# Attention sums in one step a pair, numerators and denominators as 32-column products

## The chip, the cores and the metric

The program runs on one core of one Trainium2 chip. The metric is the device time of one execution in microseconds; the kernel before has a median of 1244.84 us over three runs (1244.61 to 1248.21).

## What is computed

Attention with random features over 8 batches, 8 heads, 576 tokens and 64 dimensions, and then a gated feed-forward layer over the 4608 tokens (512 to 1536 and back to 512). Cut to what matters here:

```python
proj = einsum('bhsd,df->bhsf', x, w_phi)              # 64 -> 128 features, for q and for k
proj = proj - max(abs(proj), axis=-1, keepdims=True)
q_p, k_p = concatenate([exp(proj), exp(-proj)])       # 256 features a token
kv  = einsum('bhsf,bhsd->bhfd', k_p, v)               # sums over keys
z   = sum(k_p, axis=2)
num = einsum('bhsf,bhfd->bhsd', q_p, kv)              # numerators
den = einsum('bhsf,bhf->bhs', q_p, z)[..., None] + 1e-06
attn = num / den
out  = (silu(x @ w_gate) * (x @ w_val)) @ w_out       # x is attn, heads side by side
```

## The kernel before

Two heads make a pair; there are 32 pairs (8 batches of 4). A pair's keys are projected in three groups (`GROUPS`: two, two and one tile of 128 tokens; the last tile holds the 64 left-over tokens of both heads). For each group PE writes the projections into a PSUM bank, DVE takes the largest absolute value (L449) and subtracts it (L454) into a buffer `kp`, and ACT makes exp(x) and exp(-x) of it (L458, L459). Then PE sums over the keys (L472): the exponentials are the stationary operand, 64 features at a time into the upper or the lower half of the partitions of the bank `ps_kv`, and the values with two columns of ones (66 columns, `D2`) are the moving one. The three groups share two buffers of `kp`, and each group has a step of its own on PE. ACT copies `ps_kv` into `kvs` (L494) so that for each head a block of 128 columns holds 64 columns of kv and 64 equal columns of z.

Queries get their exponentials the same way, turned so that features lie on the partitions: in the first 8 pairs (`EARLY_PAIRS`) by products with the identity (L535), later by transposes on DVE. The numerators are four steps a pair, one for each head and half of the tokens: two products of 128x128 by 128x288 (`kvs` by exp(q) and by exp(-q)) into one bank, recorded under L313, the line of a helper through which most products go. 64 partitions of the bank hold the numerators and the other 64 the denominator, repeated. ACT copies the first into `num` (L622) and the second, plus 1e-6, into `den` (L624). DVE transposes `den` in blocks of 32 (L631), takes the reciprocal of one column of each block (L632), transposes it back, spread (L633), and multiplies (L635). The result goes on to the feed-forward layer on chip, or to `x_dram`.

The feed-forward products (L313 into `gv` and `o`, later L1008) take 12 chunks of 384 tokens. All products are float32 or split into a high and a low part of type fp32r. The last six chunks go in pairs by a scheme with seven products in place of eight, whose combined weights POOL makes (L915, L920).

The order of the instructions on each engine is not written by hand. Every step is handed to a planner (`Plan`) with its engine, a cost, a rank and what it waits for; the planner plays them through and issues them in that order. Attention steps have the better ranks, feed-forward products come last on PE and fill what is left. A step that needs a PSUM bank (`take`) starts only when one of two work banks is free (in the early pairs three more); `give` returns it. While the first feed-forward product has not begun, or a sum is open, the planner puts filler products where PE would have nothing (`nothing`, L1092 and L1096). Each engine then works strictly in that order.

## Time and profile before

| | |
|---|---|
| median of three runs | 1244.84 us |
| the profiled execution | 1244.83 us, span 1243.0 us, clock 0.998 |
| PE busy | 1215.6 us (98%) |
| DVE busy | 940.5 us (76%) |
| ACT busy | 686.3 us (55%) |
| POOL busy | 241.8 us (19%) |

One execution was recorded. Times in the profile's rows are in microseconds, unless a row says mean ns. PE is the matrix engine's products and PEld its weight loads, which overlap them; DVE, ACT and POOL are the vector, scalar and general engines. A row of groups reads: line, engine, operation, output and input tile, sizes, count, then busy time, mean ns of one, and the idle time just before them with what ended it. Busy times of PE overlap each other. A float32 product of the program appears as two records on PE. The early pairs run from 0 to some 130 us, the other 24 from about 300 to 705 us, beside feed-forward products; from about 810 us on the paired chunks run.

### The profile page before, as it was taken

The page shows a single profiled execution, that of the slowest core. Times are in us where ns is not written, and L with a number is a line of the kernel's source. Part 1 is how long each engine was busy: PE and PEld are TensorE (multiplying, and loading weights), DVE is VectorE, ACT ScalarE, POOL GpSimd, SP SyncE. Part 2 cuts the span into 40 slices and gives each one's busy share as a digit, 9 for nine tenths or more (in the row PEclk, how much of TensorE's full clock was granted, in tenths as well). Part 3 has the DMA queues.
Part 4 walks back from the last instruction along what each step waited for, and adds up shares of the span by engine and source line. Part 5 has one row for each costly group of instructions (what it writes and reads, how often), then busy time and mean ns, then how long its engine had stood idle before and what let it go on. Part 6 is the DMA issues. An engine that isn't in the chain of part 4 may idle for free.

```text
span 1243.0 us, 21611 instructions
## 1 busy us (share of the span) xinstructions
PE 1215.6 (98%) x8160; PEld 1087.3 (87%) x8160; DVE 940.5 (76%) x1674; ACT 686.3 (55%) x1419; POOL 241.8 (19%) x306
## 2 busy tenths in 40 slices
PE   8999999999999999999999999989999999999998
PEld 7777899999888888888888899979998899989997
DVE  7998799998899899999999632575658655675553
ACT  6887333336888787887887521333335433453333
POOL 0000000000000000000000010066555655565550
PEclk9999999999999999999999999999999999999999
DMA  4433444447554443444533254632223312222211
GB/s 141 137 120 98 146 178 169 174 168 219 168 159 130 130 114 110 119 123 124 152 113 97 77 189 140 190 113 66 77 73 109 124 57 72 77 102 77 77 51 51
DMA packets 107321, 149.40 MB, mean 120 GB/s; under 512 B 52048, under 2 KB 61776, under 8 KB 107216
## 3 DMA queue, kind: packets, MB, share of 16 engines
q1 hardware_dynamic: 106752, 147.76, 37.4%
q8 instruction: 64, 1.05, 0.3%
q14 instruction: 41, 0.34, 0.1%
q10 hardware_dynamic: 464, 0.26, 0.1%
HBM read 119.67 MB, written 28.31 MB: 119 GB/s over the span
## 4 chain that ended last, share of the span: by engine, by line
PE 84%; DVE 9%; DMA 3%; ACT 2%; POOL 1%; issue 1%; SPq 0%; DVEq 0%; ACTq 0%; POOLq 0%
PE gv L313 22%; PE gv L1008 19%; PE o L313 19%; PE work L313 16%; PE kv L472 5%; PE kv L313 2%; DVE m L454 1%; DVE km L449 1%; POOL a L915 1%; POOL a L920 1%; DMA w_lo<-wlo_dram 1%; DVE xl L957 1%; DVE m L953 1%; DVE m L593 0%; DVE m L633 0%
## 5 line engine op out<-in xcount | busy, mean ns | idle before, releaser
L313 PE MATMUL gv<-xh,w_hi 128*128 128x384 f32 x576 | 200.6, 348 | 2.4 <-DVE th L744 1.4
L313 PE MATMUL gv<-xh,w_lo 128*128 128x384 f32 x576 | 193.3, 336 | 0.0
L313 PE MATMUL gv<-xl,w_hi 128*128 128x384 f32 x576 | 193.2, 335 | 0.0
L1008 PE MATMUL gv<-xh,m 128*128 128x384 f32 x504 | 151.0, 338 | 3.4 <-ACT m L1016 2.6
L915 POOL TENSOR_TENSOR a<-w_hi,m 128x256 f32<-128x256 f32 x48 | 40.3, 870 | 485.5 <-DMA m<-wlo_dram 477.8
L915 POOL TENSOR_TENSOR a<-w_hi,w_lo 128x256 f32<-128x256 f32 x96 | 85.8, 924 | 192.9 <-DMA w_lo<-wlo_dram 176.0
L920 POOL TENSOR_TENSOR a<-a 128x256 f32<-128x256 f32 x144 | 115.2, 800 | 8.5
L313 PEld LDWEIGHTS gv<-xh,w_hi 128*128 128x128 f32 x576 | 108.3, 188 | 6.7 <-DVE th L744 2.0
L1019 DVE TENSOR_TENSOR a<-gv,a 128x384 f32<-128x384 f32 x72 | 39.9, 554 | 95.3 <-PE gv L1008 95.1
L313 PE MATMUL work<-m,m 128*128 128x288 f32 x408 | 110.6, 408 | 0.7 <-ACT m L624 0.7
L313 PE MATMUL o<-w_hi,hh 128*128 128x512 f32 x270 | 111.1, 411 | 0.0
L313 PEld LDWEIGHTS gv<-xl,w_hi 128*128 128x128 f32 x576 | 108.3, 188 | 3.1 <-DVE xl L659 0.2
L313 PEld LDWEIGHTS gv<-xh,w_lo 128*128 128x128 f32 x576 | 108.1, 188 | 0.0
L313 PE MATMUL o<-w_hi,hl 128*128 128x512 f32 x270 | 106.7, 395 | 0.0
L1008 PEld LDWEIGHTS gv<-xh,m 128*128 128x128 f32 x504 | 93.5, 189 | 6.4 <-ACT m L1016 3.2
L313 PE MATMUL o<-w_lo,hh 128*128 128x512 f32 x243 | 95.6, 393 | 0.0
L313 PEld LDWEIGHTS work<-m,m 128*128 128x128 f32 x408 | 75.5, 189 | 19.0 <-ACT m L624 1.0
L742 ACT ACTIVATE th<-gv 128x384 f32<-128x384 f32 x72 | 35.4, 491 | 99.5 <-PE gv L313 96.7
L767 ACT CAST hh<-th 128x384 fp32r<-128x384 f32 x108 | 55.2, 511 | 51.9 <-DVE th L747 39.4
L1008 PE MATMUL gv<-xh,w_hi 128*128 128x384 f32 x216 | 72.8, 337 | 5.0 <-DVE a L1019 5.0
L744 DVE SCALAR_TENSOR_TENSOR th<-th,gv 128x384 f32<-128x384 f32 x72 | 39.5, 548 | 46.1 <-ACT th L742 45.5
L768 DVE TENSOR_TENSOR hl<-th,hh 128x384 fp32r<-128x384 f32 x108 | 66.5, 618 | 8.7 <-ACT hh L767 8.4
(179 smaller groups left out, 2927.7 us busy)
## 6 DMA issues: line engine op xcount, KB each, us to landing
w_lo<-wlo_dram SPq DMA_DIRECT2D x60, 512.0 KB, 3.6
w_lo<-wlo_dram SPq DMA_DIRECT2D x78, 256.0 KB, 3.0
wlo_dram<-w_lo SPq DMA_DIRECT2D x36, 256.0 KB, 2.0
out_dram<-osb SPq DMA_DIRECT2D x30, 256.0 KB, 2.9
a<-in_wg_dram SPq DMA_DIRECT2D x12, 512.0 KB, 3.3
a<-in_wv_dram SPq DMA_DIRECT2D x12, 512.0 KB, 3.2
a<-in_wo_dram SPq DMA_DIRECT2D x12, 512.0 KB, 3.2
m<-wlo_dram SPq DMA_DIRECT2D x12, 512.0 KB, 3.6
```

The lines of the kernel that those rows point to most:

```text
L313: nc.tensor.matmul(o, l, r, start=a, stop=z)
L449: kmax = add("DVE", dve(n * NF), lambda m=m, view=view: vec.tensor_reduce(out=m, in_=view(), axis=AX.X, op=ALU.max, apply_absolute_value=T ...
L454: vec.tensor_tensor(out=room[:, :, 1], in0=view(), op=ALU.subtract, in1=m.rearrange("p (n o) -> p n o", o=1).broadcast_to([P, n, NF]))
L472: nc.tensor.matmul(ps_kv[r, n:n + (2 if tail else 1) * D2], x[:, r], y, start=t + h + k == 0, stop=tail and k == 1)
L742: s1 = add("ACT", act(CH), lambda: nc.scalar.activation(t_, ps_gv[0][:, :CH], AF.Tanh, scale=0.5), [ends[0], th_free[j]], FIRST)
L744: s2 = add("DVE", dve(CH), lambda: nc.vector.scalar_tensor_tensor(out=t_, in0=t_, scalar=1.0, in1=ps_gv[0][:, :CH], op0=ALU.add, op1=ALU.m ...
L767: s4 = add("ACT", act(CH), lambda: nc.scalar.copy(get(hh[b]), th[j]), [made, hid_free[b]], FIRST)
L768: s5 = add("DVE", dve(CH), lambda: nc.vector.tensor_tensor(out=get(hl[b]), in0=th[j], in1=get(hh[b]), op=ALU.subtract), [s4], FIRST)
L915: gp.tensor_tensor(out=full()[:, block(n)], in0=hi[:, block(n)], in1=get(low)[:, block(n)], op=ALU.add)
L920: gp.tensor_tensor(out=x[:, block(o)], in0=x[:, block(l)], in1=x[:, block(r)], op=ALU.subtract)
L1008: nc.tensor.matmul(o[:, :CH], l, r, start=begin and i == 0, stop=i == len(terms) - 1, skip_group_check=True)
L1019: return add("DVE", dve(CH), lambda: vec.tensor_tensor(out=snap[n](), in0=bank_c[:, :CH], in1=snap[n](), op=ALU.add), after, FIRST)
```

## The change

Sums over keys: the values get one column of ones (65 columns). Each group of exponentials has its own buffer, so that all three of a pair stand side by side; a pair's sums are one step on PE, after the last exponentials, in place of three. The projections of the next pair's keys wait for that step. `kvs` holds for each of the four blocks 64 columns of kv and 32 equal columns of z (`KV`).

Numerators and denominators: one step a pair that takes two banks. The stationary operand has 32 columns, and four products write the four 32-partition strips of a bank. In the first bank, strip n holds dimensions 32(n mod 2) and on of head n div 2 for the first 512 tokens. In the second bank are the same for the last 64 tokens, and beside them the denominators: strip n holds those of head n div 2 for one half of the tokens (288). ACT then makes three copies a pair in place of eight. DVE transposes 288 columns of denominators in place of 576 and takes nine reciprocals a partition; POOL spreads them in six copies to the partitions where the numerators stand (`spread_out`), and the transpose back (now L657) and the product (L659) follow as before. The step that used to wait for the store of the previous pair's result was the copy on ACT; now the step on PE waits for it. The planner counts several banks for a step, and holds other steps that want a bank while one waits for two.

The core of the diff (left out: the lines that only put the name of a bank into a list, and some that rename):

```diff
-D2 = D + 2
+D2 = D + 1
+KV = D + 32
...
-                if s.take is not None and not self.free and not (s.early and self.extra):
+                if s.take is not None and (saved or len(s.take) > len(self.free) + (len(self.extra) if s.early else 0)):
                     held.append((key, s))
+                    saved = True
...
-            if s.take is not None:
-                self.bank[s.take] = (self.extra if s.early and self.extra else self.free).pop(0)
+            for t in s.take or ():
+                self.bank[t] = (self.extra if s.early and self.extra else self.free).pop(0)
...
+STRIPS = 350
...
-    kp = [view("m1", [2, 2, 2, NF]) for _ in range(2)]
-    kvs = [view("m2", [4 * P]) for _ in range(2)]
+    kp = [view("m1", [n, 2, NF]) for n in (4, 4, 1)]
+    kvs = [view("m2", [4 * KV]) for _ in range(2)]
...
-    rc = sb("rc", [P, NBL])
+    rc, rp = sb("rc", [P, NBL]), sb("rp", [P, NBL // 2])
...
-            kproj = add("PE", w * (pe32(width) if plain else 3 * pe(width)), project, k_ready, rk, take=key)
+            kproj = add("PE", w * (pe32(width) if plain else 3 * pe(width)), project,
+                        [*k_ready, last.get(("kv", i - 1))], rk, take=[key])
...
-            ksub = add("DVE", dve(n * NF), centre, [kmax, last.get(("kp", 3 * i + g - 2))], freeing, give=key)
+            ksub = add("DVE", dve(n * NF), centre, [kmax], freeing, give=key)
...
-            def values(t0=t0, t1=t1, room=room, tail=tail):
-                kv_open[0] = not tail
+            powers.append(e1)
+        def values():
+            for g, (t0, t1) in enumerate(GROUPS):
+                tail = t1 == 5
                 for t in range(t0, t1):
                     for h in range(1 if tail else 2):
                         for k in range(2):
-                            x = room[:, 2 * (t - t0) + h, k]
+                            x = kp[g][:, 2 * (t - t0) + h, k]
                             y = get(vf[one])[:, 4].rearrange("p h d -> p (h d)") if tail else get(vf[one])[:, t, h]
                             n = (2 * k + h) * D2
                             for r in (slice(0, P // 2), slice(P // 2, P)):
                                 nc.tensor.matmul(ps_kv[r, n:n + (2 if tail else 1) * D2], x[:, r], y,
                                                  start=t + h + k == 0, stop=tail and k == 1)
-            kv = add("PE", 2 * n * pe32(D2), values, [e1, *v_in, last.get(("kv", i - 1)), *kv_steps[-1:]], rk)
-            last["kp", 3 * i + g] = kv
-            kv_steps.append(kv)
+        kv = add("PE", 20 * pe32(D2) // 2 + STRIPS, values, [*powers, *v_in, last.get(("kvc", i - 1))], rk)
+        last["kv", i] = kv
...
-            kvc.append(add("ACT", act(4 * D), lambda ones=ones: nc.scalar.copy(
-                cut(kvs[j], ones), sums(ones)), [kv_steps[-1], *use("kvs")], rank))
-        last["kv", i] = kvc[-1]
+            def out_of_bank(ones=ones):
+                x = ps_kv[:, :4 * D2].rearrange("p (n d) -> p n d", d=D2)
+                o = kvs[j].rearrange("p (n d) -> p n d", d=KV)
+                if ones:
+                    nc.scalar.copy(o[:, :, D:], x[:, :, D:D + 1].broadcast_to([P, 4, KV - D]))
+                else:
+                    nc.scalar.copy(o[:, :, :D], x[:, :, :D])
+            kvc.append(add("ACT", act(4 * (KV - D if ones else D)), out_of_bank, [kv, *use("kvs")], rank))
+        last["kvc", i] = kvc[-1]
...
-        copied, nu = [], None
-        for h in range(2):
-            for part in range(2):
-                key = ("n", i, h, part)
-                c = slice(part * SH, (part + 1) * SH)
-                ra, rb = rows(h)
-                def numerators(key=key, h=h, c=c):
-                    o = work[plan.bank[key]][:, :SH]
-                    terms = []
-                    for k in range(2):
-                        n = slice((2 * k + h) * P, (2 * k + h + 1) * P)
-                        terms.append((kvs[j][:, n], (qe, qx)[k][j][:, h, c]))
-                    matmuls([(o, l, r, m == 0, m == len(terms) - 1) for m, (l, r) in enumerate(terms)])
-                nu = add("PE", 2 * pe32(SH), numerators, [*done[h], *kvc, nu], rn, take=key)
-                free = last.get(("num", i - 1), ())
-                copied.append(add("ACT", act(SH), lambda key=key, ra=ra, c=c: nc.scalar.copy(
-                    num[ra, c], work[plan.bank[key]][ra, :SH]), [nu, *free], freeing))
-                copied.append(add("ACT", act(SH), lambda key=key, ra=ra, rb=rb, c=c: nc.scalar.activation(
-                    den[ra, c], work[plan.bank[key]][rb, :SH], AF.Copy, bias=1e-6), [nu, *free], freeing, give=key))
+        free = last.get(("num", i - 1), ())
+        keys = [("n", i, n) for n in range(2)]
+        WIDE = 4 * P
+        def numerators():
+            oa, ob = (work[plan.bank[key]] for key in keys)
+            strips = lambda o, c, l, x, n, begin, final: nc.tensor.matmul(
+                o[32 * n:32 * n + 32, c], l, x, start=begin, stop=final)
+            for k in range(2):
+                for n in range(4):
+                    at = (2 * k + n // 2) * KV + 32 * (n % 2)
+                    strips(oa, slice(0, WIDE), kvs[j][:, at:at + 32], (qe, qx)[k][j][:, n // 2, :WIDE],
+                           n, k == 0, k == 1)
+            for k in range(2):
+                for n in range(4):
+                    at = (2 * k + n // 2) * KV + 32 * (n % 2)
+                    strips(ob, slice(SH, SH + S - WIDE), kvs[j][:, at:at + 32], (qe, qx)[k][j][:, n // 2, WIDE:],
+                           n, k == 0, False)
+                for n in range(4):
+                    at = (2 * k + n // 2) * KV + D
+                    strips(ob, slice(0, SH), kvs[j][:, at:at + 32],
+                           (qe, qx)[k][j][:, n // 2, (n % 2) * SH:(n % 2 + 1) * SH], n, False, k == 1)
+        nu = add("PE", pe32(WIDE) * 2 + pe32(SH) * 2 + 300 + STRIPS, numerators, [*done[0], *done[1], *kvc, *free], rn, take=keys)
+        c_den = add("ACT", act(SH), lambda: nc.scalar.activation(
+            den[:, :SH], work[plan.bank[keys[1]]][:, :SH], AF.Copy, bias=1e-6), [nu], freeing)
+        c_num = [add("ACT", act(S - WIDE), lambda: nc.scalar.copy(
+            num[:, WIDE:], work[plan.bank[keys[1]]][:, SH:SH + S - WIDE]), [nu], freeing, give=keys[1])]
+        c_num.append(add("ACT", act(WIDE), lambda: nc.scalar.copy(num[:, :WIDE], work[plan.bank[keys[0]]]), [nu], freeing, give=keys[0]))
         last["kvs", i] = last["nu", i] = nu
-        turned = qe[j][:, 0]
+        turned = qe[j][:, 0, :SH]
         wide = lambda t: t.rearrange("p (a j) -> p a j", j=32)
-        t0 = add("DVE", dve(S), lambda: vec.transpose(turned, den), [*copied, *done[0], *done[1]], rt)
-        t1 = add("DVE", 260, lambda: vec.reciprocal(rc, wide(turned)[:, :, 0]), [t0], rt)
+        half = NBL // 2
+        t0 = add("DVE", dve(SH), lambda: vec.transpose(turned, den[:, :SH]), [c_den], rt)
+        t1 = add("DVE", 210, lambda: vec.reciprocal(rp, wide(turned)[:, :, 0]), [t0, last.get(("rc", i - 1))], rt)
+        def spread_out():
+            for u in range(2):
+                nc.gpsimd.tensor_copy(rc[:, u * half:(u + 1) * half], rp)
+            for h in range(2):
+                for u in range(2):
+                    n = 32 * (2 * h + u)
+                    r = 32 * (2 * h + 1 - u)
+                    nc.gpsimd.tensor_copy(rc[r:r + 32, u * half:(u + 1) * half], rp[n:n + 32])
+        ts = add("POOL", 6 * 230, spread_out, [t1, last.get(("num'", i - 1))], rt)
+        last["rc", i] = ts
         t2 = add("DVE", dve(S), lambda: vec.transpose(
-            wide(den), rc.rearrange("p (a o) -> p a o", o=1).broadcast_to([P, NBL, 32])), [t1], rt)
-        t3 = add("DVE", dve(S), lambda: vec.tensor_tensor(out=num, in0=num, in1=den, op=ALU.mult), [t2], rt)
+            wide(den), rc.rearrange("p (a o) -> p a o", o=1).broadcast_to([P, NBL, 32])), [ts], rt)
+        t3 = add("DVE", dve(S), lambda: vec.tensor_tensor(out=num, in0=num, in1=den, op=ALU.mult), [t2, *c_num], rt)
+        last["num'", i] = t2
```

How the order changes. PE at an early pair, from the numerators on; `o` and `work` are banks, `kv` the bank of the sums, `ident` the products that turn the next queries. Before:

```order
L313 MATMUL o_126<-m_0_104,m_0_105 128x288 x2
L313 MATMUL o_128<-m_0_104,m_0_105 128x288 x2
L313 MATMUL work_132<-m_0_104,m_0_105 128x288 x2
L313 MATMUL o_127<-m_0_104,m_0_105 128x288 x2
L472 MATMUL kv<-m_0_105,m_0_104 64x66 x16
L535 MATMUL o_126<-ident,m_0_105 128x128 x4
L472 MATMUL kv<-m_0_105,m_0_104 64x66 x16
L313 MATMUL o_128<-wbd,m_0_105 128x256 x2
```

Now:

```order
L614 MATMUL o_127<-m_0_104,m_0_105 32x512 x8
L614 MATMUL work_134<-m_0_104,m_0_105 32x64 x4
L614 MATMUL work_134<-m_0_104,m_0_105 32x288 x4
L614 MATMUL work_134<-m_0_104,m_0_105 32x64 x4
L614 MATMUL work_134<-m_0_104,m_0_105 32x288 x4
L478 MATMUL kv<-m_0_105,m_0_104 64x65 x32
L478 MATMUL kv<-m_0_105,m_0_104 64x130 x4
L538 MATMUL o_129<-ident,m_0_105 128x128 x4
```

Four wide steps have become one of 24 narrow products, and the three pieces of sums, which other products parted, stand together behind it.

PE at the sums of the last pair, among feed-forward products (`o` with 512 columns). Before:

```order
L313 MATMUL o_126<-w_hi_87,hl_121 128x512
L472 MATMUL kv<-a_1_2616,m_0_104 64x66 x32
L313 MATMUL o_127<-w_hi_87,hh_119 128x512
L313 MATMUL o_127<-w_lo_97,hh_119 128x512
L313 MATMUL o_127<-w_hi_87,hl_121 128x512
L472 MATMUL kv<-a_1_2616,m_0_104 64x132 x4
L313 MATMUL o_128<-w_hi_87,hh_119 128x512
```

Now:

```order
L316 MATMUL o_127<-w_hi_86,hl_121 128x512
L478 MATMUL kv<-a_1_2767,m_0_104 64x65 x32
L478 MATMUL kv<-a_1_2767,m_0_104 64x130 x4
L316 MATMUL o_128<-w_hi_86,hh_119 128x512
L316 MATMUL o_128<-w_lo_96,hh_119 128x512
```

Over all pairs the sums stood in 85 such pieces before and stand in 32 now. Behind the last numerators there were 551 feed-forward products ahead of the first paired chunk (L1008 before, L1033 now); now there are 194. Filler products ahead of the first feed-forward product number 40 in place of 26.

DVE at the denominators of a late pair; `rc` and `rp` hold reciprocals, `km` and `work` belong to the keys of another pair, `th` and `gv` to the feed-forward layer. Before:

```order
L631 STREAM_TRANSPOSE m_0_104<-m_0_105 128x576
L449 TENSOR_REDUCE km_108<-work_133 128x4
L454 TENSOR_TENSOR m_0_104<-work_133,km_108 128x4x128
L449 TENSOR_REDUCE km_109<-work_132 128x4
L454 TENSOR_TENSOR m_0_104<-work_132,km_109 128x4x128
L449 TENSOR_REDUCE km_106<-work_133 128x1
L632 RECIPROCAL rc<-m_0_104 128x18
L633 STREAM_TRANSPOSE m_0_105<-rc 128x576
L635 TENSOR_TENSOR m_0_105<-m_0_105 128x576
```

Now:

```order
L643 STREAM_TRANSPOSE m_0_104<-m_0_105 128x288
L644 RECIPROCAL rp<-m_0_104 128x9
L452 TENSOR_REDUCE km_106<-work_133 128x1
L457 TENSOR_TENSOR m_0_104<-work_133,km_106 128x128
L769 SCALAR_TENSOR_TENSOR th_117<-th_117,gv_130 128x384
L657 STREAM_TRANSPOSE m_0_105<-rc 128x576
L659 TENSOR_TENSOR m_0_105<-m_0_105 128x576
```

Between the reciprocal and the transpose back, where nearly nothing stood, there are now mostly three to ten instructions of other work, while POOL spreads the reciprocals; at three pairs there are none or one.

More of the change, by code (lines that the diff above doesn't have):

```diff
@@ L535, in turn @@
                             nc.tensor.transpose(o[:, (h * w + t) * P:(h * w + t + 1) * P], y[:, 2 * t + h], ident)
-                tn = add("PE", u * 108, turn, [qc], rank, take=key2)
+                tn = add("PE", u * 108, turn, [qc], rank, take=[key2])
                 last["qy", n] = tn
@@ L564, in project @@
                         matmuls([(acc, wst_hi, x, True, False), (acc, wst_lo, x, False, True)])
[L566 removed]
+                    pj = add("PE", 2 * pe(SH), project, [lo], rq, take=[key])
                     copies.append(add("ACT", act(SH), lambda h=h, c=c, key=key: nc.scalar.copy(
```

22 lines of the change are left out of this document (6 added, 16 removed).

## The prediction

> **What bounds the kernel now.** I first read the page's busy times and chain, then the table by stage, then the waits inside the attention stage, and last the order of time on PE, for the price of a single product. All come from one profiled execution: 1244.83 us, of which the span is 1243.0. The median of the runs shown is 1244.84 us, so the sum below is made against 1244.8.
>
> The page's busy times and the engines of its chain of waits, then the table by stage:
>
> ```profile
> PE 1215.6 (98%) x8160; PEld 1087.3 (87%) x8160; DVE 940.5 (76%) x1674; ACT 686.3 (55%) x1419; POOL 241.8 (19%) x306
> PE 84%; DVE 9%; DMA 3%; ACT 2%; POOL 1%; issue 1%; SPq 0%; DVEq 0%; ACTq 0%; POOLq 0%
> ```
> ```profile
> 150.00:300.00 150.00, 150.00 (x832) 145.08 (x831) 137.69 (x264) 59.82 (x110) 0.59 (x5) 1.00 0.52 182
> 300.00:705.00 405.00, 400.18 (x3411) 341.13 (x3410) 374.12 (x716) 321.18 (x702) 0.00 (x0) 1.00 0.43 127
> 705.00:810.00 105.00, 105.00 (x549) 97.70 (x548) 39.65 (x64) 27.69 (x52) 9.98 (x13) 1.00 0.51 165
> ```
>
> In the second fence the columns are the stretch, its length, the busy time of PE, PEld, DVE, ACT and POOL, the granted clock, the DMA share and GB/s. From 300 to 705 us 24 of the 32 pairs run among the feed-forward products; PE works 400.18 of 405 us, at full clock. DVE is not far behind with 374.12 (92%), so I ask whether anything makes PE wait there:
>
> ```profile
> PE work L313 <- ACT m L624: 2.3, 2, 1.6
> PE work L313 <- DVE a L554: 1.3, 3, 0.7
> PE kv L472 <- ACT m L458: 0.5, 1, 0.5
> PE work L313 <- DVE m L454: 0.2, 1, 0.2
> ```
>
> Those are all of PE's waits in the 405 us, 4.3 us together. From 705 to 810 us PE still works through products of the last chunk without a break while DVE is idle for 65 us. So the feed-forward work is a reserve that fills PE whenever attention is late: time saved on PE is time saved, as long as that reserve lasts.
>
> **What an attention product costs.** Busy times of PE overlap, so I take distances between starts. In order of time, on PE, at an early and at a late pair (start, us from first start to last end, what, count):
>
> ```profile
> 33.59 2.10 PE L313 MATMUL o<-m,m 128*128 128x288 f32 x8
> 35.53 1.13 PE L313 MATMUL work<-m,m 128*128 128x288 f32 x4
> ...
> 39.23 1.16 PE L472 MATMUL kv<-m,m 128*64 128x66 f32 x32
> 40.32 1.13 PE L313 MATMUL o<-wbd,m 128*128 128x256 f32 x4
> ...
> 42.46 0.67 PE L472 MATMUL kv<-m,m 128*64 128x132 f32 x8
> 43.06 1.13 PE L313 MATMUL work<-wbd,m 128*128 128x256 f32 x4
> ```
> ```profile
> 678.02 0.34 PE L313 MATMUL gv<-xh,w_lo 128*128 128x384 f32 x1
> 678.20 0.39 PE L313 MATMUL o<-w_hi,hh 128*128 128x512 f32 x1
> 678.43 0.39 PE L313 MATMUL o<-w_lo,hh 128*128 128x512 f32 x1
> 678.66 0.40 PE L313 MATMUL o<-w_hi,hl 128*128 128x512 f32 x1
> 678.99 2.09 PE L472 MATMUL kv<-m,m 128*64 128x66 f32 x64
> 681.01 0.50 PE L313 MATMUL o<-w_hi,hh 128*128 128x512 f32 x1
> 681.34 0.39 PE L313 MATMUL o<-w_lo,hh 128*128 128x512 f32 x1
> ```
>
> A float32 product of the program shows as two records. Numerators (L313, 288 columns): eight records take 35.53 - 33.59 = 1.94 us, 0.2425 each, 0.84 ns a column. Eight products a pair are 16 records: **3.88 us a pair**.
>
> The sums over keys (L472) use 64-column weights in the two halves of the array. 32 records take 1.09 us (40.32 - 39.23) and 64 take 2.02 (681.01 - 678.99); the extra 32 cost 0.93, so two records together take 0.058 us. One alone would need 66 x 0.84 = 0.055, so the two halves run side by side. 16 such waves are 0.93, which leaves 0.16 us of the 1.09 as an edge inside the run. Before it 678.99 - 678.66 is 0.33 where 0.23 is usual, behind it 681.34 - 681.01 is again 0.33: 0.10 more on either side. **A run of narrow products costs 0.36 us beside its waves.** Waves of 132 columns check this: (0.60 - 0.16) / 4 = 0.11.
>
> **The change, part by part.**
>
> Sums over keys. The same 36 products with 65 columns for 66 and 130 for 132: 32 x 0.8 + 4 x 1.6 ns = 0.03 us a pair, 1 us in all. The three steps of a pair stood in the order as 85 runs; now there are 32. 53 runs fewer x 0.36 = **19.1 us of PE**.
>
> Numerators and denominators. Away go 16 records of 0.2425 us. In come 24 products, 48 records, each in one of four 32-column strips: 512 columns (two accumulation terms, two records each: four waves), 288 (four waves) and 64 (four waves). With all four strips side by side a wave lasts as one record: 4 x 512 x 0.84 ns = 1.72 us, 4 x 0.2425 = 0.97. For the 64-column waves the trace gives two bounds: the length of the stream, 0.056 us, and four slots of the 0.029 us that a record of L472 takes on average, 0.116; four waves are 0.22 to 0.46, and I take the middle, 0.34. One run's edge, 0.36 (between 0.16, if only the part inside it recurs, and 0.72, if four strips fill and drain as two pairs). Sum 3.39 us; saved 3.88 - 3.39 = 0.49 a pair, **15.7 us** for 32. With the bounds it is 0.12 less or more for the waves, and 0.36 less or 0.20 more for the edge.
>
> The Trainium skill ("TensorE: Matmul & The Clock Gate", section "Wait — 56ns, not 53.3ns?") says that the time from start to start never drops below about 25 ns, however few columns a product has. By that a 64-column wave would be an estimated 100 ns, 0.40 us for the four, and the gain 2 us smaller; the smallest mean here is the 29 ns of L472, above that floor, so no row speaks against it.
>
> PE in all: 19.1 + 1 + 15.7 = 35.8 us. Three quarters (24 pairs) fall into the stage from 300 us, where PE is full: 26.9. The other 9.0 fall into the first 150 us. There the order has 14 more filler products of 256 columns (40 for 26) before the first feed-forward product, 14 x 0.215 = 3.0 us; I count 6.0. **26.9 + 6.0 = 32.9; 1244.8 - 32.9 = 1212 us.**
>
> What the other engines get. Here are the rows for ACT, DVE and POOL that price it:
>
> ```profile
> L624 ACT ACTIVATE m<-work 64x288 f32<-64x288 f32 x102 | 41.3, 405 | 1.4
> L622 ACT COPY m<-work 64x288 f32<-64x288 f32 x102 | 40.1, 393 | 30.6 <-PE work L313 27.3 <-DMA x_dram<-m 1.8
> L494 ACT COPY m<-kv 128x256 f32<-128x256 f32 x64 | 24.0, 375 | 9.5 <-PE kv L472 8.8
> L543 ACT ACTIVATE m<-o 128x512 f32<-128x512 f32 x32 | 17.4, 593 | 4.8 <-PE o L535 4.8
> L631 DVE STREAM_TRANSPOSE m<-m 128x576 f32<-128x576 f32 x32 | 24.7, 773 | 20.7 <-ACT m L624 20.6
> L632 DVE RECIPROCAL rc<-m 128x18 f32<-128x18 f32 x32 | 8.4, 263 | 0.7
> L298 POOL MEMSET m<- 128x20 f32 x1 | 0.1, 121 | 0.0
> L302 POOL MEMSET m<- 64x64 f32 x4 | 0.5, 146 | 0.0
> L920 POOL TENSOR_TENSOR a<-a 128x256 f32<-128x256 f32 x144 | 115.2, 800 | 8.5
> ```
>
> ACT: eight copies, 4 x 405 + 4 x 393 = 3.19 us, become three of 288, 64 and 512 columns, 0.41 + 0.25 + 0.59 = 1.25 us (the middle one between nothing and the 0.375 of L494). 62 us less, which nothing waits for: hidden. DVE: the transpose of L631 halves, 773 to 400-450 ns; about 0.33 us a pair, 11 us in all, also off the path. POOL gets six copies of nine columns a pair. The nearest rows are the fills, 0.12 to 0.15, so 0.7 to 0.9 us a pair; the far row, 800 ns, would make 4.8. DVE's second transpose waits for them, and behind it in DVE's queue stand the next group's maximum and subtraction, on which PE's projections wait. What covers it: in the early pairs three rows of DVE stand between the reciprocal and that transpose, mostly four to ten later, 1.2 us at least and usually 3 or more. Three pairs have none or one, a loss of about 1 us of DVE each, which I leave out. Without cover it would be 1 us a pair on DVE, and the late stage has (405 - 374) / 24 = 1.3 us to spare.
>
> New waits on PE. The one step of sums waits for all of a pair's exponentials; what is late then is the last group's. It can only hold feed-forward products behind it, and the order has put more of them ahead: 357 of them (551 products behind the last numerators before, 194 now) have moved up into the attention stage, 357 x 0.19 us (from 0.175 and 0.23 in the rows above) = 68 us. So the pairs come slower but DVE is less dense there, (374 - 8 + 18) of 446 us, 86%. The numerators now wait themselves for the previous pair's store, for which only ACT waited before: 1.8 us in all in the row of L622. I take 0 and keep 2 for the range. The products left, 194 x 0.19 = 37 us, must cover the preparation of the next stage; POOL's first part of it ran 16 to 22 us behind 705, where attention ends, so the cover holds:
>
> ```profile
> 720.86 3.13 POOL L915 TENSOR_TENSOR a<-w_hi,m 128x256 f32<-128x256 f32 x4 [438.58 <-DMA m<-wlo_dram]
> 723.96 3.19 POOL L920 TENSOR_TENSOR a<-a 128x256 f32<-128x256 f32 x4
> ```
>
> **The rivals.**
>
> *Two strips at a time.* This is the slower case. If the two records of a product keep their place in line, a product's second record overlaps only the next product's first, and a product costs one record's length: eight of each kind, 8 x (0.431 + 0.056 + 0.2425) = 5.84, with the edge 6.2 us for 3.88. That is 2.3 x 32 = 74 us lost against 20 gained: **1299 us**. For it: the trace has never more than two products side by side. Against it: with two halves the waves take the full two-fold, without a first or last record alone. The strips' work one after the other is 11.67 us; it becomes a loss when fewer than 11.67 / (3.88 + 0.62 - 0.36) = 2.8 run at once. Chance 0.09.
>
> *Three at a time*, a limit on how fast four streams are read: 11.67 / 3 + 0.36 = 4.25, 0.37 x 32 = 12 us lost, 20 gained: **1237**. The rows show a read rate of two streams only. Chance 0.10. The Trainium skill (same page, section "Part 3: Packing small matmuls — row/col tiling") has three column strips at 512 columns at 2.38-fold; four at that share would be an estimated 1230 us, and no row here speaks to it.
>
> *DVE becomes the bound.* Then only its 11 us come off: **1234**. For it the 92%; against it the 105 us of reserve and only 2 us of PE's waits on DVE or its chain in the late stage. Chance 0.10.
>
> *The POOL step holds DVE* at the far price, 4.8 us a pair less about 2 of cover, 2.8 x 24 = 67 us against 31 to spare and 33 gained: **1248**. Chance 0.04.
>
> *The change does not do what it says*: in the order PE has 32 single steps of each kind, so that is ruled out but for the strips above.
>
> **How the numbers follow.** The forecast, 1212, has 0.63; its own range is 1199 (both bounds in favour, no loss to fillers) to 1229 (three quarters of both against, 11.5, and the early 6.0 lost). Better than that has 0.04. To leave out no more than 2 in 10 the range reaches to the cases at 1230 to 1237: **1198 to 1240**. About 0.3%, 3.7 us, is what a measurement of this kernel can tell from no change. Faster: 0.63 + 0.04 + 0.10 + nearly all of 0.10 = 0.86; the same 0.04; slower 0.10.
>
> **What would show it.** Starts of the 32x512 records in fours some 10 ns apart, with 0.43 us from four to four, and a numerators step of 3.0 to 3.6 us; pairs of starts there show the two-strip rival. 64 runs of narrow products instead of 85. ACT busy 62 us lower, DVE 11. PE's waits from 300 us to the end of attention still under 10 us. DVE's wait for POOL at the second transpose under 0.3 us a pair. The start of L1008's products some 33 us earlier than 810. The prediction is wrong if the strips' waves are longer than 0.5 us, or if PE waits for the sums step in the late stage by more than 0.5 us a pair.

## The result

The changed kernel takes 1209.28 us (median of four runs, 1208.30 to 1209.88), the kernel before 1245.29 beside it (1244.61 to 1248.21): **ratio 0.9706, 95% interval 0.9688 to 0.9723**. The forecast was 1212. Run again later, the unaltered changed kernel came to 1208.74 (five runs, 1207.49 to 1209.76).

The page of the changed kernel: busy times, and the engines of the chain of waits.

```profile
PE 1178.2 (98%) x9198; PEld 1027.5 (85%) x9198; DVE 931.8 (77%) x1674; ACT 615.9 (51%) x1259; POOL 289.0 (24%) x498
PE 89%; DVE 6%; POOL 2%; DMA 1%; issue 1%; ACT 1%; SPq 0%; DVEq 0%; POOLq 0%
```

PE is still the bound: its share of the chain rose from 84 to 89%, and its busy time fell by 37.4 us, about as much as the time did. ACT lost 70.4 us, DVE 8.7, POOL gained 47.2.

Where the 36 us came from is read at two places that both kernels have: the feed-forward product into `gv` that has a hundred ahead of it (called the hundredth from here on), where the early pairs are over, and the first product of the paired chunks. In order of time on PE, before:

```profile
140.83 0.34 PE L313 MATMUL gv<-xl,w_hi 128*128 128x384 f32 x1
...
809.71 0.40 PE L313 MATMUL o<-w_hi,hl 128*128 128x512 f32 x1
809.95 0.34 PE L1008 MATMUL gv<-xh,w_hi 128*128 128x384 f32 x1
```

and after:

```profile
141.33 0.34 PE L316 MATMUL gv<-xl,w_hi 128*128 128x384 f32 x1
...
775.71 0.39 PE L316 MATMUL o<-w_hi,hl 128*128 128x512 f32 x1
775.93 0.33 PE L1033 MATMUL gv<-xh,w_hi 128*128 128x384 f32 x1
```

**The early pairs gained nothing (141.33 for 140.83), all of the gain to 776 us came behind them: 34.0 us.** Another 2.5 us lie in the paired stage, by the spans of the two recorded executions (1243.0 and 1206.5 us); what they come from was not followed up. The second recorded execution of the changed kernel has the early place at 140.44, so half a microsecond there is within what executions differ by. The late stage as a whole, in the table by stage (stretch, length, busy time of PE, PEld, DVE, ACT, POOL, clock, DMA share, GB/s), before and after:

```profile
282.00:810.00 528.00, 523.18 (x4054) 455.47 (x4053) 427.72 (x807) 360.91 (x777) 10.23 (x16) 1.00 0.46 139
```
```profile
282.00:776.00 494.00, 493.25 (x4824) 407.68 (x4823) 420.13 (x807) 308.21 (x657) 43.88 (x161) 1.00 0.49 148
```

The stage is shorter by 34 us at the same clock, PE works 493.25 of 494 us, and DVE, now 85% of its stage, does not hold it. All of PE's waits there are this one row:

```profile
PE o L316 <- DVE hl L793: 0.7, 1, 0.7
```

The steps themselves, in order of time on PE around one pair of the late stage (all 48 narrow records of the step are one row, named after the first):

```profile
501.10 0.34 PE L316 MATMUL gv<-xh,w_lo 128*128 128x384 f32 x1
501.37 3.12 PE L614 MATMUL work<-m,m 128*32 128x512 f32 x48
504.42 0.44 PE L316 MATMUL gv<-xh,w_hi 128*128 128x384 f32 x1
504.70 0.34 PE L316 MATMUL gv<-xl,w_hi 128*128 128x384 f32 x1
```

The step takes 504.42 - 501.37 = 3.05 us; entering costs 0.10 more (0.27 from start to start where 0.17 is usual) and leaving about as much (0.28). So a pair's numerators and denominators are **3.25 us**, forecast 3.39, before 3.88. The starts inside it, in ns from the first, taken from the trace's records:

```
512 columns:    0    7   13   20 |  453  460  467  473 |  882 ... | 1312 ...
 64 columns: 1741 1747 1754 1761 | 1797 ...
288 columns: 1852 1859 1866 1872 | 2095 ...
```

Four strips start 7 ns apart, and from four to four it is 429 ns at 512 columns, 243 at 288, 56 at 64: each four lasts as long as one record, so all four strips run side by side.

### The profile page after: what moved, and what is told of

Same layout as the page of the kernel before. It is cut to its first block, busy times and chain, and to the rows that moved or that the text cites. A ratio compares the mean times of both kernels' runs of the same rounds, so it can differ in the third digit from the quotient of the medians.

```text
span 1206.5 us, 23676 instructions
## 1 busy us (share of the span) xinstructions
PE 1178.2 (98%) x9198; PEld 1027.5 (85%) x9198; DVE 931.8 (77%) x1674; ACT 615.9 (51%) x1259; POOL 289.0 (24%) x498
## 4 chain that ended last, share of the span: by engine, by line
PE 89%; DVE 6%; POOL 2%; DMA 1%; issue 1%; ACT 1%; SPq 0%; DVEq 0%; POOLq 0%
PE gv L316 25%; PE gv L1033 20%; PE o L316 19%; PE work L316 10%; PE work L614 6%; PE kv L478 5%; PE kv L316 2%; PE o L614 1%; DVE km L452 1%; DVE m L457 1%; DMA a<-in_wg_dram 1%; DVE m L527 1%; POOL rc L653 1%; DVE km L522 1%; POOL a L940 0%
## 5 line engine op out<-in xcount | busy, mean ns | idle before, releaser
L316 PE MATMUL gv<-xl,w_hi 128*128 128x384 f32 x576 | 194.0, 337 | 0.4 <-DVE xl L684 0.4
L1033 PE MATMUL gv<-xh,m 128*128 128x384 f32 x504 | 151.0, 338 | 2.8 <-ACT m L1041 2.8
L648 POOL COPY rc<-rp 128x9 f32<-128x9 f32 x64 | 15.3, 273 | 529.4 <-DVE rp L644 529.4
L945 POOL TENSOR_TENSOR a<-a 128x256 f32<-128x256 f32 x144 | 117.7, 817 | 8.5
L316 PE MATMUL o<-w_hi,hh 128*128 128x512 f32 x270 | 108.4, 401 | 0.0
L1033 PEld LDWEIGHTS gv<-xh,m 128*128 128x128 f32 x504 | 93.6, 189 | 5.4 <-ACT m L1041 3.4
L614 PE MATMUL work<-m,m 128*32 128x288 f32 (+2 forms) x1280 | 80.4, 398 | 2.6 <-DVE m L457 2.6
L1033 PE MATMUL gv<-xh,w_hi 128*128 128x384 f32 x216 | 72.8, 337 | 3.9 <-DVE a L1044 3.8
L1033 PE MATMUL gv<-xl,m 128*128 128x384 f32 x216 | 72.9, 338 | 0.0
L1033 PE MATMUL gv<-xl,w_hi 128*128 128x384 f32 x216 | 72.7, 337 | 0.0
L614 PEld LDWEIGHTS work<-m,m 128*32 128x32 f32 x1280 | 30.7, 110 | 47.5 <-issue 30.5
```

Source lines behind the costliest of these rows:

```text
L316: nc.tensor.matmul(o, l, r, start=a, stop=z)
L614: strips = lambda o, c, l, x, n, begin, final: nc.tensor.matmul(o[32 * n:32 * n + 32, c], l, x, start=begin, stop=final)
L648: nc.gpsimd.tensor_copy(rc[:, u * half:(u + 1) * half], rp)
L945: gp.tensor_tensor(out=x[:, block(o)], in0=x[:, block(l)], in1=x[:, block(r)], op=ALU.subtract)
L1033: nc.tensor.matmul(o[:, :CH], l, r, start=begin and i == 0, stop=i == len(terms) - 1, skip_group_check=True)
```

## The experiments

Times stand beside runs of the kernel before on the same chip (1242 to 1250 us), ratios to these. "Early" is the start of the hundredth product into `gv` (140.8 before, 141.3 after). "Late" is from the 800th of them to the first product of the paired chunks (528.3 before, 494.1 after). Both are read from one recorded execution of each kernel. The edits are cut to their core; `...` marks lines left out.

**1. Sums alone.** Sums in one step, a buffer for each group of exponentials, 65 columns; numerators as before. Against the changed kernel:

```diff
-                        [*k_ready, last.get(("kv", i - 1))], rk, take=[key])
+                        [*k_ready, last.get(("kv1", i - 1))], rk, take=key)
...
-        nu = add("PE", pe32(WIDE) * 2 + pe32(SH) * 2 + 300 + STRIPS, numerators, [*done[0], *done[1], *kvc, *free], rn, take=keys)
+                nu = add("PE", 2 * pe32(SH), numerators, [*done[h], *kvc, nu], rn, take=key)
...
```

> Only the first half of the change: a pair's sums over keys in one step, a buffer for each group, 65 columns; numerators, copies and denominators as before. In the order the narrow runs on PE fall from 70 to 32 (47 to 24 behind the first 150 us), fillers at the start rise from 29 to 46. Theory A (PE's time is what is saved, in the late stage alone): 23 runs x 0.36 + 0.75 for the columns = 9 us, so about 1236 us (1233 to 1239). Theory B (the merged step saves nothing, since PE then waits for the last group's exponentials): 1243 to 1248. Theory C (the sums step carries most of the change, as the prediction's 19.1 + 1 us had it): 1225 to 1230.

1228.59 us, ratio 0.9865 (0.9843 to 0.9886). Late 510.2, 18.1 less; early 143.7, 2.8 more. Of the 18.1 the sums' own records make 7.4 (64.0 to 56.6 us from start to start), and 24 fewer runs at 0.20 for entering and leaving 4.8; 5.9 are left, by which the wide products between them stand closer. The time falls into the range of theory C, but not by its sum: C had 20 us from the sums themselves, and here they gave 12.2 in the late stage, helped by the 5.9 that no theory had.

**2. Strips alone, priced too dear.** Numerators as in the change; the sums stay three steps, with a buffer for each group, but the planner counted them dearer (2142 ns for a large group, 798 for the small one). The price, against the kernel before:

```diff
...
-            kv = add("PE", 2 * n * pe32(D2), values, [e1, *v_in, last.get(("kv", i - 1)), *kv_steps[-1:]], rk)
+            kv = add("PE", (2 if tail else 8) * pe32(D2) + STRIPS, values, [e1, *v_in, last.get(("kvc", i - 1)), *kv_steps[-1:]], rk)
```

> Only the second half: numerators and denominators as one step of 32-column products with the POOL copies, the sums over keys again in three steps (with a buffer for each group and 65 columns). Theory A: (3.88 - 3.25) x 24 = 15 us of PE in the late stage, and 4 to 8 us of small stalls there that go with the eight copies and their banks: about 1225 us (1220 to 1230). Theory C: 1229 to 1233, since the strips were to bring 15.7 us in all.

1258.51 us, ratio 1.0102 (1.0073 to 1.0131): about 1% slower, which neither theory had, though the strips took the same time as in the changed kernel. The recorded execution is the fastest of the four (1253.86). PE waits in it from 282 to 820 us, the largest:

```profile
PE work L316 <- DVE a L555: 8.9, 11, 1.6
PE work L316 <- ACT m L632: 7.8, 7, 2.0
PE work L316 <- DVE m L457: 3.2, 5, 0.9
PE kv L474 <- ACT m L461: 1.9, 1, 1.9
```

All rows of that view add up to 25 us, in a stage that has 4.3 before and 0.7 after. Feed-forward products that could have filled them were left over: 579 lay behind the last numerators. The planner believed PE busier with attention than it was, and so, by this reading, put too few of them in between. A run with the price right tests it:

**3. Strips alone, rightly priced.** As 2, with 1246 and 798 ns. Against experiment 2:

```diff
-            kv = add("PE", (2 if tail else 8) * pe32(D2) + STRIPS, values, [e1, *v_in, last.get(("kvc", i - 1)), *kv_steps[-1:]], rk)
+            kv = add("PE", (2 if tail else 4) * pe32(D2) + STRIPS, values, [e1, *v_in, last.get(("kvc", i - 1)), *kv_steps[-1:]], rk)
```

> As the kernel with the strips alone, which took 1258.5 us with some 39 us more stalls on PE behind 282 us, but with the sums' steps priced at 1246 and 798 ns in place of 2142 and 798. Theory K: the stalls fall with the price, 1222 to 1235 us. Theory M: without the merged step the pairs stay too dense, 1248 to 1260.

1221.54 us, ratio 0.9806 (0.9791 to 0.9821): theory K, half a microsecond below its range. 37 us lie between two kernels that do the same work, by one number of the planner. Late 500.9, 27.5 less; early 145.9, 5.1 more. PE's waits in the late stage are gone:

```profile
PE o L316 <- ACT osb L837: 0.4, 1, 0.4
PE work L316 <- ACT m L568: 0.3, 1, 0.3
```

So each part gains by itself, 17 and 24 us, 41 together for the 36 of both: the closing up of wide products, some 6 us, is in either, and is had once.

**4. The price alone.** Whether the change's gain is merely a better price for the sums: the kernel before, with 1246 and 798 ns in place of 1792 and 448. Against the kernel before, the whole edit:

```diff
-            kv = add("PE", 2 * n * pe32(D2), values, [e1, *v_in, last.get(("kv", i - 1)), *kv_steps[-1:]], rk)
+            kv = add("PE", (2 if tail else 4) * pe32(D2) + 350, values, [e1, *v_in, last.get(("kv", i - 1)), *kv_steps[-1:]], rk)
```

> The kernel before with one number changed: the cost that the planner counts for a step of sums goes from 1792 and 448 ns to 1246 and 798, near what the trace shows for such a run. No instruction is added or removed; in the order attention is spread over more feed-forward products (about 300 behind the last numerators for 528). Theory K (the change gained part of its time because the planner's price of the sums came closer to the chip, so that PE meets fewer late operands): the 9 us of stalls that the kernel with the sums alone lost go here too, 1233 to 1239 us. Theory M (it is the merged step itself and its single set of buffers that spaces the pairs): 1242 to 1248.

1244.43 us, ratio 0.9993 (0.9982 to 1.0004): nothing, as theory M had it. Late 522.8, 5.5 less; early 145.3, 4.5 more.

**5. Strips in line.** The same 24 products, those of one strip one after the other, to see whether the four run side by side because of the order in which they are issued. Against the changed kernel, and the same for the second bank:

```diff
-            for k in range(2):
-                for n in range(4):
+            for n in range(4):
+                for k in range(2):
...
```

> As the changed kernel, but the products of one strip follow one another: strip 0 with both terms, then strip 1, and so on. Same products, same sums. If PE starts products strictly in the order of the program, a strip's products run one behind the other and only neighbours of two strips overlap: about 13 records of 0.43 us for 512 columns, some 10 us a step for 3.05, 24 x 6.8 = 160 us or more: 1360 to 1430 us, starts no longer in fours. If every strip takes its products on its own, nothing changes: 1207 to 1211 us, starts in fours.

1261.65 us (a single execution). The step, in order of time on PE:

```profile
502.06 0.39 PE L316 MATMUL o<-w_hi,hl 128*128 128x512 f32 x1
502.38 4.98 PE L614 MATMUL work<-m,m 128*32 128x512 f32 x48
507.29 0.45 PE L316 MATMUL gv<-xh,w_hi 128*128 128x384 f32 x1
```

4.91 us for 3.05, and 24 x 1.86 = 44.6 is what the late stage grew by (538.6 for 494.1); early is 150.7, 9.4 more. Neither theory holds. The starts, again in ns:

```
512 columns:    0   13   26   40 |  453  466  480  493 |  882 ... | 1311 ...
then:        1740 1796 1852 2095 | 2337 2343 2393 2423 2449 2479 2691 2721 | 2964 2970 ... | 3590 3596 ... | 4217 4273 4329 4571
```

In the first bank, where each strip has four records, all four strips still run side by side, though in the program the first strip's four records stand ahead of the second strip's first. In the second bank each strip has eight records; there only two run together, and the next strip's first record starts with the fifth of the strip ahead (2337 and 2343, 2964 and 2970). Five stretches of about 0.6 us take the place of two. As far as these starts tell (the trace does not name a record's strip), a strip takes up to four records ahead of their turn, and the fifth holds all that is behind it.

**6. POOL's copies doubled.** The order of the change; each of the six copies made twice. Against the changed kernel:

```diff
-            for u in range(2):
-                nc.gpsimd.tensor_copy(rc[:, u * half:(u + 1) * half], rp)
-            for h in range(2):
...
+            for again in range(2):
+                for u in range(2):
+                    nc.gpsimd.tensor_copy(rc[:, u * half:(u + 1) * half], rp)
+                for h in range(2):
...
```

> As the changed kernel with the same order on PE, DVE and ACT, but POOL makes its six copies twice a pair (1.5 us more). Theory P (DVE's wait for POOL is what took the gain of the first 150 us away): DVE waits 1.2 to 1.5 us longer in each of the 8 early pairs, 8 to 12 us later at the end of them, and in the late stage the reserve hides it: 1217 to 1222 us. Theory D (the early pairs are held by DVE's own work and the weights' arrival, POOL is beside the path): under 3 us more, 1208 to 1212.

1221.89 us, ratio 0.9812 (0.9794 to 0.9831). Early 152.1, 10.8 more than the change; late 497.8, only 3.8 more: theory P. DVE's waits for POOL and PE's for DVE in the whole span:

```profile
DVE m L658 <- POOL rc L654: 28.3, 20, 2.7
PE o L538 <- DVE m L527: 12.4, 8, 2.7
```

Up to the hundredth product DVE waits 14.0 us for POOL where the change has 3.9, so the 10.1 more are nearly all of the delay. In the early pairs the way from reciprocal to product is on the path; in the late stage feed-forward products cover it nearly whole.

**7. Four copies.** DVE's reciprocal writes each partition's nine values twice, and POOL makes only the four copies between strips. Against the changed kernel:

```diff
...
-        ts = add("POOL", 6 * 230, spread_out, [t1, last.get(("num'", i - 1))], rt)
+        ts = add("POOL", 4 * 230, spread_out, [t1, last.get(("num'", i - 1))], rt)
```

> As the changed kernel, but the reciprocal writes both halves itself and POOL makes four copies a pair in place of six (and is priced at four). The doubled copies cost 10.8 us in the 8 early pairs and 3.8 behind them. Theory P (the way over POOL lies on the early pairs' path, 0.27 us a copy): 8 x 2 x 0.27 = 4 us less there and about 1 us later, 1203 to 1206 us. Theory D (the early pairs end no sooner than the weights and DVE allow): 1207 to 1211.

1208.13 us (1208.01 to 1212.06), ratio 0.9701 (0.9685 to 0.9717): no difference from the change, where theory P had 1203 to 1206. Early 142.2, late 494.2. The recorded execution is the slowest of the four, with 14 us of the early pairs at half clock where the change has 7, so its early place says little. But the other three took 1208.0 to 1208.3 us at a granted clock of 0.996 to 0.997, and the change 1208.3 to 1208.7 at 0.996: at the same clock, too, the way from reciprocal to transpose, shorter by 0.35 us a pair, gains about half a microsecond.

**8. POOL dearer to the planner.** 2400 ns for 1380. Against the changed kernel:

```diff
-        ts = add("POOL", 6 * 230, spread_out, [t1, last.get(("num'", i - 1))], rt)
+        ts = add("POOL", 6 * 400, spread_out, [t1, last.get(("num'", i - 1))], rt)
```

> As the changed kernel, but the planner counts 2400 ns for POOL's six copies in place of 1380, so that more of DVE's other work stands between the reciprocal and the transpose back (five or six rows in the early pairs for three). DVE's waits for POOL there, 3.9 us before 134 us, go. If what costs is DVE's lost time, 1204 to 1207 us; if it is the length of the way over POOL itself, it stays, 1207 to 1212.

1212.66 us, ratio 0.9739 (0.9724 to 0.9754). DVE's waits for POOL halve (3.2 us for 6.3), and still some 3 us are lost: early 145.1, 3.8 more; late 494.0. The way from the reciprocal's end to the transpose grew to 2.6 us on average of the eight early pairs, from 2.1.

**9. One copy.** The order of the change, but one copy of 18 columns in place of six; no value goes to another strip, so the quotients are not the reference's. Against the changed kernel:

```diff
...
-            for u in range(2):
-                nc.gpsimd.tensor_copy(rc[:, u * half:(u + 1) * half], rp)
...
+            nc.gpsimd.tensor_copy(rc.rearrange("p (o a) -> p o a", o=2),
+                                  rp.rearrange("p (o a) -> p o a", o=1).broadcast_to([P, 2, half]))
```

> The changed kernel with the same order on every engine, but POOL makes one copy a pair in place of six (each partition's nine reciprocals twice side by side, with no move between partitions, so the quotients are wrong where a reciprocal should come from another strip). POOL's step falls from 1.5 us a pair to about 0.3 to 0.6. Theory P (the hop over POOL is what holds the early pairs, as doubling the copies cost 10.8 us there): the 100th product into gv begins 6 to 10 us before 141.3, the late stage does not move, 1200 to 1204 us. Theory N (doubling only made a hop that just fits too long; the early pairs are held by something else, as the kernel with four copies says): the 100th product into gv begins within 3 us of 141.3, 1207 to 1211 us. In both, DVE's waits for POOL at the second transpose fall below 2 us.

1204.0 us, ratio 0.9664 (0.9648 to 0.9681). Early 137.1, **4.2 less than the change**; late 494.7. Between both theories: with all but one copy gone the early pairs gain some 4 us, not 6 to 10.

**10. Copies on two engines, and the change once more.** As 7, but two of the four copies on ACT. Against experiment 7:

```diff
...
+        ts = [add(e, 2 * c, lambda e=e, h=h: spread_out(e, h), [t1, last.get(("num'", i - 1))], rt)
+              for h, (e, c) in enumerate((("POOL", 270), ("ACT", 200)))]
```

> The changed kernel with a shorter hop and right quotients: DVE's reciprocal writes each partition's nine values twice side by side, and of the four copies between strips POOL makes two and ACT two, side by side; the planner counts 540 ns for POOL's and 400 ns for ACT's. Theory P (the length of the hop holds the early pairs: one copy in place of six gave 4.2 us there): the hop falls from 1.5 to some 0.6 us a pair, the 100th product into gv begins 2 to 4 us before 141.3, the late stage stays within 2 us, 1204 to 1207 us. Theory O (another order in the early pairs is worth as much, or ACT's queue holds its two copies): 1207 to 1212 us, with DVE waiting at its second transpose for ACT's copy.

> The changed kernel once more, unaltered, as the measure for the kernel with the copies on two engines: both theories 1208 to 1211 us. Theory H (the half-clock windows come from thin use of PE in the early pairs and fall by chance): other windows than at 107.1 and 127.6 us, and the 100th product into gv within 2 us of 141.3.

1209.03 us (1207.34 to 1211.31; ratio 0.9697, 0.9676 to 0.9718) against 1208.74 (0.9695, 0.9676 to 0.9714): the same. The way from the reciprocal's end to the transpose fell from 2.1 to 1.1 us on average of the eight early pairs, and DVE waited for ACT's copy once, 0.7 us; early is 141.2 all the same. In its chain of waits from 20 to 141 us POOL makes 1%, against 7.5 in the change, and PE 56 against 38: PE holds it again. What took it back is seen, as far as one execution tells, in the table by stage, for two copies on ACT, for the change, for one copy and for the kernel before:

```profile
20.00:134.00 114.00, 100.27 (x1231) 74.56 (x1223) 96.90 (x193) 72.28 (x179) 4.77 (x16) 0.93 0.38 109
```
```profile
20.00:134.00 114.00, 99.85 (x1232) 73.06 (x1224) 96.41 (x191) 68.10 (x163) 13.59 (x48) 0.97 0.36 109
```
```profile
20.00:134.00 114.00, 101.73 (x1259) 75.77 (x1252) 100.33 (x199) 69.36 (x165) 2.43 (x8) 0.99 0.39 116
```
```profile
20.00:134.00 114.00, 107.32 (x982) 84.92 (x981) 100.31 (x194) 86.65 (x204) 0.00 (x0) 1.00 0.37 111
```

The granted clock, third from the end, is 0.93: here PE ran 17 us at half clock, in the change 7, with one copy 3, before none. At the same granted clock over the whole run, 0.994, the one execution with copies on two engines took 1207.3 us and two of the change 1209.2 and 1209.9. The half-clock windows of the change's second execution (from 105.5 and 126.0 us) stand 1.6 us from those of the first (107.1 and 127.6), so they do not fall at random, as theory H had it. But their number need not be the same in every execution: the nine of the change have granted clocks from 0.993 to 0.996.

None of these beats the changed kernel with right quotients by more than the runs can tell.

## Why the prediction held, and where it did not

The time is 2.7 us from the forecast, and the mechanism of the late stage, which carries most of it, was right. That the total came so near is in part luck: the early pairs failed by 6.5 us, and 9.5 us came from where the forecast had nothing.

| | forecast | measured |
|---|---|---|
| early pairs | -6.0 | +0.5 |
| late stage, sums | -15.1 | -12.2 |
| late stage, numerators | -11.8 | -15.1 |
| late stage, wide products closer | 0 | -7 |
| paired stage | 0 | -2.5 |

The measured column is read from the two recorded executions.

**What bounds the kernel.** Right: time saved on PE in the late stage was time saved. The products left behind the last numerators were to cover the next stage with 37 us; the last record of the numerators began at 739.1 us, and the paired chunks 36.8 later without a wait of PE.

**Sums over keys: the term was mis-sized in both factors.** The 85 pieces counted rows of the order, some of which stood side by side. Counted as unbroken runs of narrow products there were 70 before, 47 of them in the late stage. The sums' runs there fell by 24, not by three quarters of 53. But each was worth more than 0.36: in experiment 1 the late stage's sums and their edges gave 12.2 us, of which 0.75 are the columns, so 0.48 a run. The 0.16 us inside a run, read off one place, was too low for the average run.

**Numerators and denominators.** The four waves of 512 and 288 columns came as worked out (429 and 243 ns). The 64-column waves were mis-sized: 56 ns each, the lower bound, in place of the middle, 85. The edge was right: 3.05 less the waves' 2.91 leaves 0.14 inside, with 0.20 outside 0.34, for 0.36. Together 0.63 us a pair in place of 0.49. The Trainium skill ("TensorE: Matmul & The Clock Gate", section "Wait — 56ns, not 53.3ns?") has no start closer than about 25 ns to the last; here the 64-column records come four in 56 ns, 14 ns each, so the trace does not agree for strips. The kernel before had shown as much: record by record, its sums at 678.99 us start 6 to 7 and some 52 ns apart in turn. The 29 ns that the prediction took for a slot, and against which it saw no row speak for a floor of 25, is the mean of these two. Of its 2.38-fold for three strips (same page, "Part 3: Packing small matmuls — row/col tiling") this run shows a better case: four strips together take 429 ns, as long as one record of 512 columns.

**Two or three strips at a time.** Wrong for the order of the change. Experiment 5 shows what that rival would have needed: when one strip's eight records follow one another, two run together, and the kernel comes to 1262.

**The late stage gained 7 us that no step had.** Wide products stand closer by that much. PE's listed waits, 4.3 us before and 0.7 after, are half of it. Sums alone and strips alone show 6 of it each, by the same balance, so either change of the order brings it; what the other half consists of stays open.

**Early pairs: the step that failed.** The forecast took 9.0 us off PE there less 3.0 of fillers. The products did get shorter by 10.5 us (sums 28.8 to 24.5, numerators 34.1 to 27.9, from start to start up to the hundredth product), and the fillers cost 2.6. But 4.5 came back as gaps among the projections and 3.8 among the first feed-forward products. PE was not full there: a chain over DVE and POOL set the end. Of the chain of waits from 20 to 141 us PE makes 60% before and 38% in the changed kernel, DVE 24 and 43%, POOL nothing and 7.5%. Two of its rows in the changed kernel:

```profile
51.89 0.69 POOL rc L653
53.07 0.79 DVE m L657
```

In order of time, that place on DVE and POOL:

```profile
50.58 0.22 DVE L644 RECIPROCAL rp<-m 128x9 f32<-128x9 f32 x1
50.92 0.60 POOL L648 COPY rc<-rp 128x9 f32<-128x9 f32 x2 [11.53 <-DVE rp L644]
51.58 1.45 POOL L653 COPY rc<-rp 32x9 f32<-32x9 f32 x4
53.07 0.78 DVE L657 STREAM_TRANSPOSE m<-rc 128x576 f32<-128x576 f32 x1 [0.53 <-POOL rc L653]
```

From the end of the reciprocal to the transpose it is 2.3 us, where nearly nothing lay before. The copies were mis-sized, by the nearest rows (fills of 0.12 to 0.15 us):

```profile
L648 POOL COPY rc<-rp 128x9 f32<-128x9 f32 x64 | 15.3, 273 | 529.4 <-DVE rp L644 529.4
L653 POOL COPY rc<-rp 32x9 f32<-32x9 f32 x128 | 30.3, 237 | 5.9
L657 DVE STREAM_TRANSPOSE m<-rc 128x576 f32<-128x576 f32 x32 | 24.7, 773 | 6.4 <-POOL rc L653 6.3
```

2 x 273 + 4 x 237 ns are 1.5 us a pair, not 0.7 to 0.9. DVE waited 6.3 us for them in all, 0.2 a pair, which is under the 0.3 foreseen, and far from the rival in which POOL holds DVE. But more than half of it fell in the early pairs, six times, where three pairs in all were expected to have too little cover (DVE's waits from 0 to 141 us):

```profile
DVE m L657 <- POOL rc L653: 3.9, 6, 1.4
```

Experiments 6 and 9 bear this out from both sides at an unchanged order: twice the copies 10.8 us later, one copy 4.2 us earlier, with the late stage as it was and 1204.0 us in all. (Experiment 6 ran 17 us at half clock up to there, the change 7.) But 1.6 of these 4.2 are the window at half clock from 127.6 us, which the kernel with one copy does not have. In the chains of waits of the change and of that kernel, the same 21 feed-forward products:

```profile
127.54 5.49 PE gv L316 x21
```
```profile
124.89 3.93 PE gv L316 x21
```

That leaves 2.6 us, and whether the window follows from the hop is not shown. Of the two kernels with right quotients and a shorter hop, both planned anew, that of experiment 10 ran 17 us at half clock, and that of experiment 7 gained half a microsecond at the same clock, where 0.35 us for each of eight pairs would be 2.8. So the hop is shown to lie on the path of the early pairs, but its price there is not settled. What the other 2 us of the failed 6.5 are is open too: in all the kernels that were run, but for the one copy, the hundredth product came between 140.4 and 152.1 us, and with the price alone 4.5 us late, so 2 us are within what an order of the early pairs does by itself.

**The other engines.** ACT: the copies gave 63 us as worked out (0.41 + 0.21 + 0.61 us a pair for 3.19); of the other 7.4 the smaller copies of the sums, which the forecast had not counted, are 3.3 (24.0 before, 11.9 + 8.8 now):

```profile
L496 ACT COPY m<-kv 128x256 f32<-128x256 f32 x32 | 11.9, 372 | 33.8 <-PE kv L478 33.5
L494 ACT COPY m<-kv 128x128 f32<-128x128 f32 x32 | 8.8, 274 | 0.0
```

DVE: the transpose fell from 773 to 466 ns; the sum is 8.7 for 11. DVE did not become the bound (85% of the late stage, forecast 86%), and the store of the previous pair's result held no numerators. That PE waits for the sums' step, the other thing that would have made the forecast wrong, came to 0.2 us in the whole span.

## What to carry to other kernels

Count the runs of narrow products that are unbroken in the order, not its rows, and price a saving stage by stage: where another engine's chain sets the end, a shorter product only moves a gap. When products are packed into strips, issue one product of each strip in turn, and not all of one strip first. And when work is planned by costs, price a changed step as the trace shows it: a step that was counted 2142 ns in place of 1246 turned a gain of 24 us into a loss of 13.

## What the runs showed of the hardware

**Half clock follows a half-idle window.** In the changed kernel, in stretches of 3.4 us ahead of and within the two early windows (the clock is third from the end):

```profile
103.80:107.10 3.30, 1.51 (x33) 0.76 (x34) 3.23 (x7) 2.94 (x6) 0.00 (x0) 1.00 0.47 159
107.10:110.50 3.40, 3.30 (x10) 2.37 (x10) 3.30 (x9) 2.58 (x8) 0.29 (x2) 0.50 0.04 3
124.20:127.60 3.40, 1.61 (x7) 1.08 (x7) 2.20 (x5) 1.70 (x5) 0.00 (x0) 1.00 0.39 87
127.60:131.00 3.40, 3.40 (x11) 3.40 (x12) 0.54 (x1) 0.00 (x0) 0.00 (x0) 0.50 0.16 58
```

PE was busy 46 and 47% of a stretch, and the next one ran at half clock, although it had work nearly throughout. All stretches at half clock in the thirteen executions recorded, from 18 us on and but for one that the program's end cuts off, last a multiple of 3.413 us and lie on one grid in each. There are 42 of them, and by that grid all begin after a window in which PE was busy 55% or less by its records (12% the least); no window under 44% was followed by full clock; between 45 and 55% both happen. The Trainium skill ("TensorE: Matmul & The Clock Gate", section "Part 1: The HAM clock gate (the "warmup" mystery)") has a free-running window of 3413 ns, and the trace agrees; it has the clock fall after an idle window, and here one no more than about half busy did. This was read off thirteen traces, and no run was made to force it. It is one way in which a stage with thin work on PE costs more than its gaps: in the window from 127.6 the feed-forward products start 0.32 us apart in place of 0.17.

**Strips take work ahead of their turn**, by the starts of experiment 5 up to four records, which is two float32 products of a strip. Other numbers of products per strip were not run.

**A tiny copy on POOL costs about a quarter of a microsecond**, 237 ns for 32 partitions by 9 and 273 for 128 by 9, and 317 in experiment 9 for 128 by 18: by these three most of it is there whatever the size. It is not fixed: the same 32 by 9 took 216 ns in experiment 6, and 343 in experiment 10, where ACT made its copies at the same time.
